# Beta as one table of 128 rows of 12 numbers: one load in place of three, one set of gate instructions in place of two

## The chip, the cores and the metric

The kernel runs on one core of a Trainium2 chip. The metric is the device time of one execution in microseconds (us); lower is better. A core has a matrix engine (PE, whose weight loads are shown apart as PEld), a vector engine (DVE), a scalar engine (ACT), a general engine (POOL) and a queue engine (SP), which here only issues DMAs. 16 DMA engines move the data between device memory (DRAM) and the core's on-chip memory, which has 128 rows called partitions.

## The reference

Four batches, eight heads, 576 positions, head size 64. Attention with a causal mask is mixed, by a gate for each head, with a read from a memory matrix; the result, 2304 tokens of 512 numbers, goes through a two-layer network with a squared ReLU.

```
scores = q @ k.T / sqrt(D), causal;  a = softmax(scores);  local = a @ v
q_p = phi(q)                              # phi(x) = (x if x > 0 else exp(x) - 1) + 1
mem_out = (q_p @ M_prev) / (q_p @ z_prev + 1e-6)
g = 1 / (1 + exp(-beta))                  # beta: one number for each of the 8 heads
attn = g * mem_out + (1 - g) * local
out = relu(x @ w_in) ** 2 @ w_out         # x: attn as [2304, 512]; w_in 512x2048, w_out 2048x512
```

The inputs arrive in 64-bit floats for the two weight matrices and in 32-bit floats for the rest. The host may lay inputs out anew; it does no arithmetic.

## The kernel before, in words

The whole program is one stream of work for each engine. A scheduler that runs while the program is built orders the instructions of every engine; the source fixes what depends on what, and the order is written out by the scheduler, so a change in one place can move instructions in others.

**First tokens.** `first_tokens` (L229) computes the attention output of positions 0 to 63 of all four batches, in two groups `g` of two batches. The list `SEQ` (L56) says in which order SP issues the loads of this stage: `a0` and `b0` (L250, L252, L254: q, k, rows of q, and z for group 0, into `tr`), `g` (`load_beta`, L116, which also emits the gate arithmetic), `a1` (group 1), `r` (one weight load, L197, into `raw`), `b1`, `r`, `c0` (L258: v and M for group 0), `l` (the loads of the first attention pair, L340, L344, L347), `r`, `r`, `c1`.

All these DMAs sit in one queue. Eight completion semaphores are used in rotation, so that from the ninth on each DMA is held back until the one issued eight places earlier has landed.

**Beta.** Before the change, `gp` has four columns: partitions 0 to 63 hold the even heads, partitions 64 to 127 the odd heads, so L117 and L118 each read four numbers that lie two apart in DRAM, for 64 partitions. `gm` has all eight heads on all 128 partitions (L119). `gates` (L127) forms 1/(1+exp(-beta)) in both tiles by an exponential on ACT (L129), an addition (L130) and a reciprocal (L131) on DVE for each; then come `gi`, `gm` as 1/(1-g), `gs`, `gpb` and `g1b` on DVE (L132 to L139). `gpb` and `g1b` are used by the first tokens (L283, L298), `gi`, `gm` and `gs` by the attention that follows (L438, L528, L410).

**phi of a group** (L271 to L284): exponential on ACT (L276), minimum on DVE (L277), then L278, L279, L280 to L283 on DVE, and L284 on POOL.

**Weights.** Each 512 KB piece of weights is loaded as raw 64-bit words into one of a few buffers (L197), turned into two 32-bit parts by L167, L169 and L173 on DVE with L168 and L172 on ACT between them (`split_weight`), and kept on chip.

**The rest.** `attention` (L350) works on pairs of heads; `moe` (L607) takes a block of 256 tokens, multiplies by `w_in` into `up` (L631 to L633) and by `w_out` into `oacc` (L621 to L623), each product in three parts. Attention of later pairs runs between the blocks of `moe`. The last stretch is `moe` alone.

Of the kernel before, what the change touches and what calls it, by code (L numbers as in the profile page):

```python
# [8 lines left out]
F32 = mybir.dt.float32  # L9
# [4 lines left out]
AF = mybir.ActivationFunctionType  # L14
ALU = mybir.AluOpType
AX = mybir.AxisListType

B, H, S, D = 4, 8, 576, 64
NP = H // 2
DM, FF = 512, 2048  # L20
NTOK = B * S
P = 128
# [68 lines left out]
def fused_kernel(ctx: ExitStack, tc: tile.TileContext, t0_d, zt_d, kk_d, qv_d, beta, w_in, w_out, out):  # L91
    nc = tc.nc
    w_in = w_in.bitcast(U32)
    w_out = w_out.bitcast(U32)
    cp = ctx.enter_context(tc.tile_pool(name="cp", bufs=1))
# [13 lines left out]
    nc.gpsimd.affine_select(  # L109
        out=mask, in_=mask, pattern=[[-1, MW]], compare_op=ALU.is_ge, fill=-1e30, base=448, channel_multiplier=1  # L110
    )
    gp = cp.tile([P, NP], F32, name="gp")
    gm = cp.tile([P, H], F32, name="gm")
    b2 = beta.rearrange("(p h) -> h p", h=2)

    def load_beta():  # L116
        nc.sync.dma_start(gp[:D], b2[0].partition_broadcast(D))  # L117
        nc.sync.dma_start(gp[D:], b2[1].partition_broadcast(D))  # L118
        nc.sync.dma_start(gm, beta.partition_broadcast(P))  # L119
        gates()  # L120

    gi = cp.tile([P, H], F32, name="gi")
# [2 lines left out]
    g1b = cp.tile([P, GN], F32, name="g1b")  # L125

    def gates():  # L127
        for t in (gp, gm):
            nc.scalar.activation(t, t, AF.Exp, scale=-1.0)  # L129
            nc.vector.tensor_scalar(out=t, in0=t, scalar1=1.0, scalar2=None, op0=ALU.add)  # L130
            nc.vector.reciprocal(t, t)  # L131
        nc.vector.reciprocal(gi, gm)  # L132
        nc.vector.tensor_scalar(out=gm, in0=gm, scalar1=-1.0, scalar2=1.0, op0=ALU.mult, op1=ALU.add)
        nc.vector.reciprocal(gm, gm)
        nc.vector.tensor_scalar(out=gs, in0=gm, scalar1=SC, scalar2=None, op0=ALU.mult)

        for b in range(GB):
            nc.vector.tensor_copy(gpb[:, b * NP : (b + 1) * NP], gp)
        nc.vector.tensor_scalar(out=g1b, in0=gpb, scalar1=-1.0, scalar2=1.0, op0=ALU.mult, op1=ALU.add)  # L139
# [89 lines left out]
    def first_tokens(tp, ahead):  # L229
# [10 lines left out]
        for step in SEQ.split():  # L240
            if step == "r":
                ahead()
            elif step == "l":
                nxt.append(loads(*order[0]))
            elif step == "g":
                load_beta()
            else:
                g = int(step[1])
                if step[0] == "a":
                    nc.sync.dma_start(tr[g][:, : 2 * GD], t0_d[g, :, : 2 * GD])  # L250
                elif step[0] == "b":
                    nc.sync.dma_start(tr[g][:, 2 * GD : 3 * GD], t0_d[g, :, 2 * GD : 3 * GD])  # L252
                    for h in range(2):
                        nc.sync.dma_start(  # L254
                            tr[g][h * D : (h + 1) * D, 3 * GD : 4 * GD], zt_d[2 * g + h].partition_broadcast(D)
                        )
                else:
                    nc.sync.dma_start(tr[g][:, 4 * GD :], t0_d[g, :, 3 * GD :])  # L258
# [525 lines left out]
```

## Time and profile before

| what | us |
|---|---|
| three runs, median | 615.64 |
| three runs, lowest and highest | 613.45 and 617.97 |
| the profiled execution, its own time | 613.01 |
| its span, first to last instruction | 611.2 |

The span is the part of the profiled execution that the trace covers; 1.81 us of its own time lie around it. Times of single instructions and waits come from this one execution and are counted from the span's start. An idle time in square brackets behind an instruction is how long its engine stood still before it, with what ended the wait.

### The profile page before, as it was taken

The numbers are of one execution on the slowest core, as the hardware profiler recorded it, in microseconds if no ns is written. First come the engines' busy times: TensorE is split into PE (matmuls) and PEld (weight loads), VectorE is DVE, ScalarE is ACT, GpSimd is POOL, SyncE is SP. The second block draws the span as 40 slices with busy tenths as digits, with TensorE's granted clock in tenths as the row PEclk, the third lists the DMA queues.
The fourth block names the chain that finished last, engine by engine and source line by source line (L and its number), as shares of the span: only waits on it lengthen the run. The fifth ranks groups of instructions, "written<-read, shape, count | busy, mean of one in ns | idle before, by whom it ended". The sixth has DMA issues, their size and how long they took to land.

```text
span 611.2 us, 11532 instructions
## 1 busy us (share of the span) xinstructions
PE 566.8 (93%) x4198; PEld 483.2 (79%) x4198; DVE 408.5 (67%) x1287; ACT 329.5 (54%) x748; POOL 168.8 (28%) x139
## 2 busy tenths in 40 slices
PE   2268999899998999999999999999999999999997
PEld 2156887688877887888888888888888899998996
DVE  3999989766878876977788989877787611001000
ACT  1598797565557645666565555654556412312312
POOL 1420213134432433133332333332421221221221
PEclk9995999999997999999999999999999999999999
DMA  5949476576465756585554755563536310200000
GB/s 180 394 154 373 118 222 161 128 168 132 99 125 134 174 108 125 126 194 131 131 131 102 153 120 147 124 162 92 119 83 118 88 34 1 69 1 1 35 0 35
DMA packets 128120, 76.28 MB, mean 125 GB/s; under 512 B 99904, under 2 KB 113216, under 8 KB 128064
## 3 DMA queue, kind: packets, MB, share of 16 engines
q1 hardware_dynamic: 128064, 75.55, 49.8%
q8 instruction: 33, 0.54, 0.4%
q14 instruction: 23, 0.19, 0.1%
HBM read 42.63 MB, written 8.78 MB: 84 GB/s over the span
## 4 chain that ended last, share of the span: by engine, by line
PE 67%; DVE 14%; DMA 12%; ACT 3%; issue 2%; SPq 1%; POOL 0%; ACTq 0%; DVEq 0%
PE up L631 10%; PE up L633 9%; PE up L632 9%; PE oacc L621 9%; PE oacc L622 8%; PE oacc L623 8%; PE sp L468 6%; DMA aT<-a 4%; DMA vv<-in_qv_dram 3%; DVE w L173 2%; PE acc L553 2%; PE pm L435 2%; DMA raw<-in_w_in_dram 2%; DVE a L523 2%; DVE e L472 1%
## 5 line engine op out<-in xcount | busy, mean ns | idle before, releaser
L631 PE MATMUL up<-xh,w 128*128 128x256 f32 x576 | 167.3, 291 | 0.2 <-DVE vy L409 0.2
L633 PE MATMUL up<-xh,w 128*128 128x256 f32 x576 | 166.1, 288 | 0.0
L632 PE MATMUL up<-xl,w 128*128 128x256 f32 x576 | 165.9, 288 | 0.0
L646 POOL TENSOR_TENSOR gl<-r,gh 128x512 fp32r<-128x512 f32 x72 | 100.7, 1398 | 222.6 <-DVE gh L645 125.8
L631 PEld LDWEIGHTS up<-xh,w 128*128 128x128 f32 x576 | 111.0, 193 | 8.6 <-issue 4.4
L621 PE MATMUL oacc<-w,gh 128*128 128x512 f32 x288 | 115.4, 401 | 0.0
L632 PEld LDWEIGHTS up<-xl,w 128*128 128x128 f32 x576 | 111.0, 193 | 5.1 <-issue 2.6
L633 PEld LDWEIGHTS up<-xh,w 128*128 128x128 f32 x576 | 110.9, 193 | 4.5 <-issue 3.3
L622 PE MATMUL oacc<-w,gh 128*128 128x512 f32 x288 | 114.0, 396 | 0.0
L484 ACT ACTIVATE e<-e,mx 128x320 f32<-128x320 f32 (+3 forms) x128 | 77.9, 610 | 62.6 <-DVE mx L472 62.5
L623 PE MATMUL oacc<-w,gl 128*128 128x512 f32 x288 | 109.3, 394 | 0.0
L637 ACT ACTIVATE r<-up 128x512 f32<-128x512 f32 x72 | 42.6, 592 | 118.3 <-PE up L633 113.1
L639 POOL TENSOR_TENSOR r<-r 128x512 f32<-128x512 f32 x40 | 45.4, 1134 | 153.8 <-ACT r L637 153.8
L523 DVE SCALAR_TENSOR_TENSOR a<-e,a 128x128 f16<-128x128 f32 x120 | 72.3, 623 | 14.8 <-ACT a L521 14.7
L645 DVE CAST gh<-r 128x512 fp32r<-128x512 f32 x40 | 17.0, 425 | 90.1 <-ACT r L641 87.9
L472 DVE CUSTOM_DVE_ANT_0 e<-sp,mask 128x320 f32<-128x320 f32 (+3 forms) x128 | 56.6, 475 | 8.9 <-PE sp L468 8.6
L621 PEld LDWEIGHTS oacc<-w,gh 128*128 128x128 f32 x288 | 54.3, 188 | 10.4 <-issue 0.7
L622 PEld LDWEIGHTS oacc<-w,gh 128*128 128x128 f32 x288 | 54.3, 189 | 9.4 <-issue 1.0
L623 PEld LDWEIGHTS oacc<-w,gl 128*128 128x128 f32 x288 | 53.1, 188 | 10.8 <-issue 0.6
L521 ACT ACTIVATE a<-e 128x128 f16<-128x128 f32 x120 | 56.9, 521 | 1.5 <-DMA aT<-a 0.8
L553 PE MATMUL acc<-vs,aT 128*128 128x128 f16 x308 | 37.1, 220 | 0.0
L555 DVE TENSOR_REDUCE s<-acc 128x128 f32<-128x256 f32 x60 | 24.2, 417 | 18.3 <-PE acc L553 18.3
(130 smaller groups left out, 885.3 us busy)
## 6 DMA issues: line engine op xcount, KB each, us to landing
raw<-in_w_in_dram SPq DMA_DIRECT2D x11, 512.0 KB, 8.7
vv<-in_qv_dram SPq DMA_DIRECT2D x16, 320.0 KB, 3.1
raw<-in_w_out_dram SPq DMA_DIRECT2D x9, 512.0 KB, 7.1
kd<-in_kk_dram SPq DMA_DIRECT2D x16, 288.0 KB, 3.1
out_dram<-o SPq DMA_DIRECT2D x16, 256.0 KB, 2.4
xd<-memx SPq DMA_DIRECT2D x31, 128.0 KB, 2.1
xn<-xd SPq DMA_DIRECT2D x14, 256.0 KB, 2.8
qm<-in_qv_dram SPq DMA_DIRECT2D x8, 321.0 KB, 3.1
```

The costliest lines, as they stand in the source:

```text
L472: nc.vector.tensor_tensor_reduce(out=e[:n, h, ks], in0=sps[:n, h, :w], in1=mask[:n, 448 - q0 + s * w : 448 - q0 + s * w + w], scale=-0.125 ...
L484: nc.scalar.activation(e[:n, h, :ke], e[:n, h, :ke], AF.Exp, bias=bs, scale=-1.0, accum_out=sm[:n, h : h + 1])
L521: nc.scalar.mul(av[:, :, o0 : o0 + w], x, SC)
L523: nc.vector.scalar_tensor_tensor(out=av[:, :, o0 + w : o0 + 2 * w], in0=x, scalar=SC, in1=av[:, :, o0 : o0 + w], op0=ALU.mult, op1=ALU.sub ...
L553: nc.tensor.matmul(o2, aT[:, h * nb + c, :n], vs[:, h, c], start=False, stop=c == i)
L621: nc.tensor.matmul(acc[t], gh[:, u, ts], w_out_op(f, 0), start=f == 0, stop=False)
L622: nc.tensor.matmul(acc[t], gh[:, u, ts], w_out_op(f, 1), start=False, stop=False)
L623: nc.tensor.matmul(acc[t], gl[:, u, ts], w_out_op(f, 0), start=False, stop=f == NF - 1)
L631: nc.tensor.matmul(up[:, u, :], w_in_op(f, k, 0), xh[:, k, :], start=k == 0, stop=False)
L632: nc.tensor.matmul(up[:, u, :], w_in_op(f, k, 0), xl[:, k, :], start=False, stop=False)
L633: nc.tensor.matmul(up[:, u, :], w_in_op(f, k, 1), xh[:, k, :], start=False, stop=k == NK - 1)
L646: nc.gpsimd.tensor_tensor(out=gl, in0=r, in1=gh.bitcast(F32), op=ALU.subtract)
```

## The change

The host lays beta out as a table of 128 rows of 12 numbers: four for `gp` (even heads in rows 0 to 63, odd heads in rows 64 to 127) and eight for `gm`. One DMA loads the table into the tile `gpm`, of which `gp` and `gm` are now column ranges. Exponential, addition and reciprocal run once over the 12 columns. What follows in `gates` is as before.

```diff
-    gp = cp.tile([P, NP], F32, name="gp")
-    gm = cp.tile([P, H], F32, name="gm")
-    b2 = beta.rearrange("(p h) -> h p", h=2)
+    gpm = cp.tile([P, NP + H], F32, name="gpm")
+    gp, gm = gpm[:, :NP], gpm[:, NP:]
 
     def load_beta():
-        nc.sync.dma_start(gp[:D], b2[0].partition_broadcast(D))
-        nc.sync.dma_start(gp[D:], b2[1].partition_broadcast(D))
-        nc.sync.dma_start(gm, beta.partition_broadcast(P))
+        nc.sync.dma_start(gpm, beta)
         gates()
...
     def gates():
-        for t in (gp, gm):
-            nc.scalar.activation(t, t, AF.Exp, scale=-1.0)
-            nc.vector.tensor_scalar(out=t, in0=t, scalar1=1.0, scalar2=None, op0=ALU.add)
-            nc.vector.reciprocal(t, t)
+        nc.scalar.activation(gpm, gpm, AF.Exp, scale=-1.0)
+        nc.vector.tensor_scalar(out=gpm, in0=gpm, scalar1=1.0, scalar2=None, op0=ALU.add)
+        nc.vector.reciprocal(gpm, gpm)
         nc.vector.reciprocal(gi, gm)
...
+    bt = _np.asarray(inputs["beta"])
+    bt = _np.concatenate([_np.repeat(bt.reshape(NP, 2).T, D, axis=0), _np.tile(bt, (P, 1))], axis=1)
...
-        "beta": _np.ascontiguousarray(inputs["beta"]),
+        "beta": _np.ascontiguousarray(bt),
```

Lines behind the change have lower numbers afterwards: by 3 from L119 to L116, by 4 from L130 on. The scheduler writes the order anew; three places follow.

SP's queue at the start of the program, before. `tr` are the loads of the first tokens, `raw` the weights; the numbers behind names only tell buffers apart.

```order
L250 DMA tr_119<-in_t_dram 128x1024
L252 DMA tr_119<-in_t_dram 128x512
L254 DMA tr_119<-in_zt_dram 64x512 x2
L117 DMA gp<-in_beta_dram 64x4x1
L118 DMA gp<-in_beta_dram 64x4x1
L119 DMA gm<-in_beta_dram 128x8
L250 DMA tr_120<-in_t_dram 128x1024
L197 DMA raw_142<-in_w_in_dram 128x1024
L252 DMA tr_120<-in_t_dram 128x512
L254 DMA tr_120<-in_zt_dram 64x512 x2
```

The same place after the change:

```order
L246 DMA tr_118<-in_t_dram 128x1024
L248 DMA tr_118<-in_t_dram 128x512
L250 DMA tr_118<-in_zt_dram 64x512 x2
L116 DMA gpm<-in_beta_dram 128x12
L246 DMA tr_119<-in_t_dram 128x1024
L193 DMA raw_136<-in_w_in_dram 128x1024
L248 DMA tr_119<-in_t_dram 128x512
L250 DMA tr_119<-in_zt_dram 64x512 x2
```

Three DMAs of beta have become one at the same place in the queue; what stands around it is in the same order.

DVE at the gates, before (`w` and `t` belong to phi of group 0, L278 to L283):

```order
L130 TENSOR_SCALAR gp<-gp 128x4
L278 SCALAR_TENSOR_TENSOR w<-tr_119,w 128x8x64
L131 RECIPROCAL gp<-gp 128x4
L130 TENSOR_SCALAR gm<-gm 128x8
L279 TENSOR_TENSOR tr_119<-tr_119,w 128x512
L138 COPY gpb<-gp 128x4 x2
L131 RECIPROCAL gm<-gm 128x8
L280 TENSOR_REDUCE t_179<-tr_119 128x8
L139 TENSOR_SCALAR g1b<-gpb 128x8
...
L283 TENSOR_TENSOR t_179<-t_179,gpb 128x8
L135 TENSOR_SCALAR gs<-gm 128x8
L167 TENSOR_SCALAR raw_142<-raw_142 128x512
```

The same after the change (rows in the middle of either piece are left out, the same arithmetic in both):

```order
L126 TENSOR_SCALAR gpm<-gpm 128x12
L274 SCALAR_TENSOR_TENSOR w<-tr_118,w 128x8x64
L127 RECIPROCAL gpm<-gpm 128x12
L275 TENSOR_TENSOR tr_118<-tr_118,w 128x512
L128 RECIPROCAL gi<-gpm 128x8
L134 COPY gpb<-gpm 128x4 x2
L276 TENSOR_REDUCE t_173<-tr_118 128x8
...
L163 TENSOR_SCALAR raw_136<-raw_136 128x512
L278 RECIPROCAL t_173<-t_173 128x8
L131 TENSOR_SCALAR gs<-gpm 128x8
L279 TENSOR_TENSOR t_173<-t_173,gpb 128x8
```

One addition and one reciprocal are gone, the addition on beta is still ahead of L278 (L274 after the change), and the first weight piece's L167 (L163) now stands three short instructions earlier.

SP's queue later, while the last weights are loaded (`xw` and `hw` are weight pieces in borrowed buffers, `xd` and `aT` belong to attention), before:

```order
L197 DMA raw_677<-in_w_in_dram 128x1024
L574 DMA xd_92<-memx 128x2x128
L197 DMA xw<-in_w_out_dram 128x512
L197 DMA hw<-in_w_in_dram 128x1024
L197 DMA xw<-in_w_out_dram 128x512
L527 DMA_TRANSPOSE aT<-a 128x6x128
L197 DMA hw<-in_w_in_dram 128x1024
L340 DMA kd<-in_kk_dram 128x576
```

And after the change:

```order
L570 DMA xd_91<-memx 128x2x128
L193 DMA raw_671<-in_w_in_dram 128x1024
L193 DMA xw<-in_w_out_dram 128x512 x2
L523 DMA_TRANSPOSE aT<-a 128x6x128
L193 DMA hw<-in_w_in_dram 128x1024 x2
L340 DMA qm<-in_qv_dram 128x130
L340 DMA qm<-in_qv_dram 128x256
L336 DMA kd<-in_kk_dram 128x576
```

The same DMAs are there, and their order has changed: the store of `xd` is one weight piece earlier, both `xw` pieces come ahead of the transpose, and `kd` behind `qm`. From there on the order differs at many places, on PE, DVE and ACT too.

## Rows read from the trace of the kernel before

**Rows 1.** From the profile's page: busy time of the engines over the whole span; then the granted clock of PE in tenths of full speed, and the data rate, in 40 slices of 15.3 us.
```profile
PE 566.8 (93%) x4198; PEld 483.2 (79%) x4198; DVE 408.5 (67%) x1287; ACT 329.5 (54%) x748; POOL 168.8 (28%) x139
...
PEclk9995999999997999999999999999999999999999
...
GB/s 180 394 154 373 118 222 161 128 168 132 99 125 134 174 108 125 126 194 131 131 131 102 153 120 147 124 162 92 119 83 118 88 34 1 69 1 1 35 0 35
```

**Rows 2.** The chain of waits that ends at 80 us, two of its steps: start, length, what.
```profile
5.37 10.10 DMA raw<-in_w_in_dram
15.49 0.98 DVE raw L167
```

**Rows 3.** The DMA view of 0 to 13 us in 40 slices of 0.325 us, with the packets by size.
```profile
GB/s 0 0 0 0 0 101 113 176 239 365 403 410 403 391 347 177 95 7 0 0 0 1 0 0 0 1 1 0 13 14 27 40 92 216 354 391 372 442 416 403
DMA packets 1383, 1.95 MB, mean 150 GB/s; under 512 B 771, under 2 KB 771, under 8 KB 1383
```

**Rows 4.** The DMA view of 5.6 to 8.6 us.
```profile
DMA packets 306, 0.00 MB, mean 1 GB/s; under 512 B 305, under 2 KB 305, under 8 KB 306
```

**Rows 5.** The DMA issues of SP in order of time: start, length, engine, line, what, count.
```profile
2.89 0.65 SPq L117 DMA_DIRECT2D gp<-in_beta_dram  x1
3.59 0.62 SPq L118 DMA_DIRECT2D gp<-in_beta_dram  x1
4.25 0.61 SPq L119 DMA_DIRECT2D gm<-in_beta_dram  x1
4.89 0.43 SPq L250 DMA_DIRECT2D tr<-in_t_dram  x1
5.37 0.44 SPq L197 DMA_DIRECT2D raw<-in_w_in_dram  x1
5.85 1.77 SPq L252 DMA_DIRECT2D tr<-in_t_dram  x1
7.67 2.70 SPq L254 DMA_DIRECT2D tr<-in_zt_dram  x2
```

**Rows 6.** From issue to landing of the two DMAs of `gp`, from the view of that tile.
```profile
DMA to landing us min/median/max: 4.9/6.4/7.8
```

**Rows 7.** The engines in order of time, 6 to 16 us, the instructions around the gates; the idle time before and what ended it in brackets.
```profile
6.13 0.43 DVE L277 TENSOR_SCALAR w<-w 128x512 f32<-128x512 f32 x1 [3.33 <-ACT w L276]
...
11.48 0.20 ACT L129 ACTIVATE gp<-gp 128x4 f32<-128x4 f32 x1 [5.38 <-DMA gp<-in_beta_dram]
11.72 0.17 DVE L130 TENSOR_SCALAR gp<-gp 128x4 f32<-128x4 f32 x1 [5.16 <-ACT gp L129]
...
12.51 0.21 ACT L129 ACTIVATE gm<-gm 128x8 f32<-128x8 f32 x1 [0.83 <-DMA gm<-in_beta_dram]
12.75 0.17 DVE L130 TENSOR_SCALAR gm<-gm 128x8 f32<-128x8 f32 x1 [0.17 <-ACT gm L129]
12.86 0.69 DVE L279 TENSOR_TENSOR tr<-tr,w 128x512 f32<-128x512 f32 x1
...
13.82 1.97 PE L269 MATMUL sp<-tr 64*64 64x64 f32 x32 [7.36 <-DMA tr<-in_t_dram]
...
15.02 0.17 DVE L135 TENSOR_SCALAR gs<-gm 128x8 f32<-128x8 f32 x1
15.49 0.97 DVE L167 TENSOR_SCALAR raw<-raw 128x512 uint32<-128x512 uint32 x1 [0.30 <-DMA raw<-in_w_in_dram]
```

**Rows 8.** The longest waits of DVE between 15.4 and 57.9 us: what waited, for what, us in total, times, the longest.
```profile
DVE w L173 <- ACT w L172: 0.6, 1, 0.6
DVE raw L167 <- DMA raw<-in_w_in_dram: 0.3, 1, 0.3
```

**Rows 9.** Stretches of the program: length, busy us of PE, PEld, DVE, ACT and POOL (with counts), granted clock of PE as a share of full speed, DMA share, GB/s.
```profile
15.50:57.90 42.40, 22.68 (x155) 16.13 (x151) 41.20 (x106) 32.16 (x75) 11.44 (x10) 0.87 0.79 301
57.90:100.00 42.10, 41.86 (x270) 35.83 (x268) 39.44 (x108) 34.56 (x83) 10.10 (x7) 0.97 0.70 192
100.00:120.00 20.00, 16.52 (x112) 12.73 (x111) 16.56 (x61) 12.40 (x27) 3.41 (x3) 1.00 0.50 121
...
170.00:190.00 20.00, 17.19 (x126) 12.84 (x122) 16.27 (x63) 12.27 (x39) 4.66 (x5) 0.92 0.63 147
186.60:193.50 6.90, 6.73 (x32) 5.80 (x32) 6.45 (x28) 4.19 (x13) 0.00 (x0) 0.51 0.60 133
190.00:490.00 300.00, 297.15 (x2326) 253.37 (x2327) 242.13 (x791) 174.96 (x407) 89.64 (x71) 0.99 0.58 127
490.00:611.20 121.20, 117.71 (x767) 106.72 (x766) 12.05 (x27) 29.90 (x50) 26.61 (x21) 1.00 0.06 20
46.70:60.30 13.60, 10.79 (x43) 8.88 (x44) 12.50 (x38) 10.81 (x28) 0.84 (x1) 0.50 1.00 383
```

**Rows 10.** PE in order of time at the first product with `w_in`, two successive matmuls of one shape at the lower clock and two at the full clock.
```profile
59.95 0.41 PE L631 MATMUL up<-xh,w 128*128 128x256 f32 x1
60.16 0.41 PE L632 MATMUL up<-xl,w 128*128 128x256 f32 x1
...
67.02 0.28 PE L632 MATMUL up<-xl,w 128*128 128x256 f32 x1
67.14 0.28 PE L633 MATMUL up<-xh,w 128*128 128x256 f32 x1
```

## The prediction

> **What bounds the kernel now.** I read the page first. PE is busy 93% of the span, but its clock is down in the fourth of the 40 slices and partly in the thirteenth, and in the first five slices the data rate goes up and down [rows 1]. So the end is set by PE, and the start by something else. The cut by stretches shows where one passes into the other: from 15.5 to 57.9 us PE is busy 22.7 of 42.4 us and DVE 41.2; from 57.9 to 100 us PE is busy 41.9 of 42.1 us, and up to 490 us it stands still for few us in all [rows 9]. The change lies ahead of both, in the first 15.5 us. Whether a gain there reaches the end depends on two things: what ends those 15.5 us, and whether DVE, from there to 57.9, waits for anything that doesn't move with it.
>
> The chain of waits answers the first: it enters DVE's work at 15.49 with the first weight piece, which was issued at 5.37 and took 10.10 us to land [rows 2]. The DMA view shows why so long. The bytes of group 0 of the first tokens flow at some 400 GB/s up to about 5 us, then the rate falls to nothing for over 3 us and is back at 350 only at about 11 us [rows 3]. In that hole the queue is not empty: from 5.6 to 8.6 us 306 packets went through, 305 of them under 512 B [rows 4]. Those are beta. By the shapes in SP's order it is read as 2 x 64 x 4 single numbers (they lie two apart in DRAM) and 128 rows of 32 B, 640 packets in all; the whole of 0 to 13 us has 771 small ones [rows 3]. Behind beta, in the same queue, stand the loads of group 1 (issued at 4.89) and the first weight piece (5.37) [rows 5], and they get no bytes until beta is through. SP itself is held up too: the next issues take 1.77 us, and 2.70 us for two [rows 5].
>
> The time line of the engines shows the second victim. DVE is done with L277 at 6.56 and then stands still 5.16 us for the exponential of `gp`, whose data landed only at 11.48; `gm` came at 12.51, and the gates and the phi of group 0, mixed, last until L135 ends at 15.19. PE waits 7.36 us for group 1 [rows 7].
>
> **The change, part by part.**
>
> *The loads.* 640 packets become 128, one for each row of 48 B. In the hole they pass at 305 / 3.0 us = 102 per us [rows 4]. 640 of them make 6.3 us, 128 make 1.3 us; the queue behind them moves forward by 5.0 us. The rows have no packet of 48 B; bounds: the second half of `gp` (256 packets) landed at 3.59 + 7.8 = 11.4 and the first at 2.89 + 4.9 = 7.8 [rows 5, 6], so at the slowest of the 16 DMA engines 256 packets took 3.6 us, and a gain below 3.6 would mean that not even one of the three DMAs was saved; above, 6.3 if the new rows pass for nothing beside the bytes of group 0. Below that stands the case in which the hole isn't made by the packets at all (a rival, below). I take 5.0, since it comes from the hole itself.
>
> The row says that three small DMAs hold a queue for over 6 us. The Trainium skill (DMA: Bandwidth & Descriptors, "Anatomy of one DMA — SWDGE (gpsimd) path") speaks against it: about 2 us of a DMA are fixed and mostly completion, descriptor generation is small, and "You can emit a lot of descriptors before the incremental cost shows up". By that rule the three DMAs overlap and dropping two of them gives next to nothing, the rival below that leaves the hole open. The trace disagrees so far, with 4.9 and 7.8 us to landing for 1 KB each [rows 6]; the page's figure was fitted for the gpsimd path, and these come from SP.
>
> *SP.* From 2.89 to 4.89 the three issues take 2.0 us [rows 5]; one takes about 0.7, so group 1 is issued some 1.3 us sooner. That adds nothing to the 5.0: its bytes would still wait behind beta. If the hole were gone altogether, it would be the 1.3 us that count. The DMAs held back until the eighth before them has landed move with the landings.
>
> *Gates.* One exponential (0.21 us on ACT), one addition and one reciprocal on DVE go. ACT stood still 0.83 us before that exponential, so it is worth nothing. On DVE a short instruction holds the next back by 0.11 us (12.75 to 12.86) [rows 7]: 0.2 us for two. What the 12 columns cost over 4 or 8 I set at nothing: 4 and 8 columns took 0.17 us alike. A loss is here too: `gp` no longer comes 1.0 us ahead of `gm`; the first addition waits for all 12 columns, with L278 and the rest of phi queued behind it on DVE. So beta is there at 12.5 - 5.0 = 7.5, the addition starts 0.24 later as before (11.48 to 11.72), at 7.75, and the mixed work of 15.19 - 11.72 = 3.47 us, less 0.2, ends at 11.0. The first weight piece is there by 15.49 - 5.0 = 10.5; its L167 now stands three short instructions earlier, which lets it use some of that. DVE reaches its weight work at about 11.0 in place of 15.49: 4.5 us sooner. Late next is thus DVE, by 0.5 us, and no longer the data.
>
> *From 15.5 to 57.9 us.* DVE's longest waits there are 0.6 and 0.3 us [rows 8], so the stage is as long as DVE's work, which stays the same. It moves as a whole, and the first product with `w_in` goes from 57.9 to 53.4 us. From there PE carries the 4.5 us to the end.
>
> *The order.* The scheduler moves DMAs on SP while the last weights come in, and much on PE and DVE behind that. No row prices it. The nearest are the idle times that PE has in this order: 20.0 - 16.5 = 3.5 us at 100 to 120, 20.0 - 17.2 = 2.8 us at 170 to 190 [rows 9]. An order may save one of them or add one; I take nothing, with 2.8 to 3.5 us either way.
>
> *The sum.* The profiled execution took 613.01 us (span 611.2, 1.81 around it): 613.0 - 4.5 = 608.5. The median of the runs lies 2.6 above that execution, so 615.6 - 4.5 = 611.1, 0.7% less.
>
> **Rivals.**
>
> The low clock stays where it is. PE runs at half (1.2 GHz) from 46.7 to 60.3 us, after a stretch in which it was often idle [rows 9]. At that clock matmuls of 256 columns follow each other at 0.21 us (59.95 to 60.16), at the full 2.4 GHz at 0.12 us (67.02 to 67.14) [rows 10]. If the stretch doesn't move with the work, the 4.5 us of products that now come before 57.9 are done at that pace and lose 4.5 x (1 - 0.12 / 0.21) = 1.9 us: 613.0. For it: nothing shows what starts the stretch to the us. Against it: PE's idle time ahead of it moves with the work.
>
> The hole stays: it has another cause than the number of packets, or 128 rows of 48 B hold the queue as long. Then only 0.2 us go: 615.4. For it: the bytes moved are few in both. Against it: the 305 small packets in the hole, and that nothing else went through it.
>
> A better order. One of PE's idle times goes, and the low clock that follows it: from 186.6 to 193.5 us the granted clock is 0.51 [rows 9], which costs 6.9 x (1 - 0.12 / 0.21) = 3.0 us at PE's pace, with the 2.8 us of standing still 5.8. That gives 605.3. For it: such a fall comes only behind idle time, and the order is new. Against it: at 100 to 120 PE stood still longer and the clock stayed at 1.00, so the two needn't go together.
>
> A worse order, and the time is over 615.6. The place is where attention of a later pair stands in PE's queue ahead of products that could run, as at 170 to 190. One such stop more with its fall of the clock costs the same 5.8 us: 616.9. It decides from 4.5 us on, so a stop without the fall doesn't do it, and two with it give 622.7. For it: PE, DVE and SP are in a new order from about 70 us on. Against it: from 190 to 490 us PE stands still for only 2.9 us in 300 [rows 9], so there is much other work to put between.
>
> **How the numbers follow.** 1% of 615.64 is 6.2 us, about what a measurement of this kernel can tell from no change: faster is below 609.5, slower above 621.8. The forecast has 0.46, the low clock that stays 0.12, the hole that stays 0.10, the better order 0.20, the worse 0.12 (half of it two stops). Faster takes the better order and 0.12 of the forecast, where the gain of the loads is nearer to 6.3 or the order helps by a us or two: 0.32. Slower takes the two stops and 0.01 from the edge: 0.07. The same has the remaining 0.61. The predicted time is 611.1. The range goes from 604.5, below the better order, to 617.5, above one stop more; outside are the two stops and the edges of the order. The forecast's own range is 608 to 614.
>
> **What would show it.** Right: the data rate shows no hole of over 2 us between 5 and 11 us; beta lands near 7.5; the addition on beta starts near 7.8; the first weight piece is split from about 11.0 on; DVE is busy from there to the first product at about 53.4; the later stretches are as long as before within 3 us. Wrong: small packets still fill several us; or DVE is early by 4 us, but waits for data before 53; or the first product is early and the gain is gone by 200 us, with new idle time or a low clock on PE. The forecast fails above all if the later order gives or takes over 2 us.

## The result: 1.0% slower, with the start five us shorter

The changed kernel takes 622.88 us (median of 4 runs, 618.59 to 625.61), the kernel before 616.74 (median of 4 runs taken with them): a ratio of 1.0105, 95% interval 1.007 to 1.014. The forecast was 611.1 us, 604.5 to 617.5. It was wrong, and on the other side. The profiled execution of the changed kernel took 621.40 us against 613.01 before, 8.4 us more.

Its page, the same rows as in [rows 1] (busy time, granted clock and data rate in 40 slices, here of 15.5 us):

```profile
PE 571.1 (92%) x4198; PEld 484.9 (78%) x4198; DVE 409.8 (66%) x1285; ACT 330.2 (53%) x747; POOL 166.4 (27%) x139
...
PEclk9987999899998999999999999799999999999999
...
GB/s 297 374 194 247 222 178 139 122 105 133 111 146 106 144 94 164 97 169 134 154 93 151 109 112 86 149 137 116 103 82 112 83 111 10 68 1 1 35 0 35
```

The counts on PE are the same, DVE has two instructions fewer and ACT one, as the change says. The first slice moves 297 GB/s in place of 180. The granted clock has a fall that [rows 1] lack, a 7 in slice 26, near 390 us.

The start went as forecast, or better. The DMA view of 0 to 13 us, as in [rows 3], then that of 5.6 to 8.6 us, as in [rows 4]:

```profile
GB/s 0 0 0 0 0 101 139 139 277 429 391 353 391 403 391 207 226 191 252 315 366 391 391 366 378 359 359 353 252 284 277 303 290 277 334 277 391 403 429 389
DMA packets 1444, 3.60 MB, mean 277 GB/s; under 512 B 307, under 2 KB 313, under 8 KB 1444
...
DMA packets 296, 1.02 MB, mean 341 GB/s; under 512 B 26, under 2 KB 26, under 8 KB 296
```

The hole is not shorter, it is gone: the rate never falls below 190 GB/s after 3 us, and where 305 of 306 packets were small, 26 of 296 are. The same issues as in [rows 5], and the instructions that answer to [rows 7] (idle time before and its end in brackets):

```profile
2.89 0.59 SPq L116 DMA_DIRECT2D gpm<-in_beta_dram  x1
3.53 0.43 SPq L246 DMA_DIRECT2D tr<-in_t_dram  x1
4.00 0.43 SPq L193 DMA_DIRECT2D raw<-in_w_in_dram  x1
...
6.45 0.21 ACT L125 ACTIVATE gpm<-gpm 128x12 f32<-128x12 f32 x1 [0.64 <-DMA gpm<-in_beta_dram]
...
6.70 0.17 DVE L126 TENSOR_SCALAR gpm<-gpm 128x12 f32<-128x12 f32 x1 [0.42 <-ACT gpm L125]
...
9.90 0.43 DVE L163 TENSOR_SCALAR raw<-raw 128x512 uint32<-128x512 uint32 x1 [0.56 <-DMA raw<-in_w_in_dram]
...
52.53 0.56 PE L627 MATMUL up<-xh,w 128*128 128x256 f32 x1
```

Group 1 is issued at 3.53 in place of 4.89. The exponential starts at 6.45 (11.48 and 12.51 before), DVE takes up the first weight piece at 9.90 (15.49 before), and the first product with `w_in` starts at 52.53 (57.88 before): 5.35 us sooner.

So the 8.4 us, and the 5.35 on top of them, are lost behind 52.5 us. To find the place I mark the first copy out of `oacc` of each of the nine blocks of `moe`; the lengths between the marks, in us, in the profiled executions:

| kernel | start to first product | block 1 | 2 | 3 | 4 | 5 | 6 | 7 | 8 and 9 |
|---|---|---|---|---|---|---|---|---|---|
| before | 57.9 | 70.1 | 77.8 | 63.3 | 66.0 | 64.2 | 65.4 | 54.0 | 88.2 |
| changed | 52.5 | 73.4 | 78.0 | 63.9 | 64.7 | 75.6 | 59.4 | 59.5 | 88.2 |

Blocks 5 to 7 take 183.6 us before and 194.5 after. Block 1 has 3.3 us too; but that is the execution of before: the nine other profiles in before's order (e1, e3 to e6, e9, e10, e15 and e16 below) have 72.3 to 73.9 there. Its 613.01 us was a good draw, 3.7 below the median. Late in block 5 the changed kernel has a stop that before has not. Its steps on the chain of waits (start, length, what), then PE in order of time:

```profile
387.50 0.41 DVE memx L559 x2
387.90 0.02 issue
387.92 2.43 DMA xd<-memx
390.35 0.02 issue
390.37 2.59 DMA xn<-xd
392.96 0.04 issue
393.00 1.42 PE px L594 x8
```
```profile
390.12 0.23 PE L544 MATMUL acc<-vs,aT 128*128 128x128 f16 x1 [1.41 <-DMA aT<-a]
...
390.84 0.42 PE L464 MATMUL sp<-kh,qh 64*128 64x320 f32 x2
393.00 1.42 PE L594 MATMUL px<-identr,xn 128*128 128x128 f32 x8 [1.74 <-DMA xn<-xd]
```

The last rows of an attention are stored to `xd` and fetched back as `xn` for the next block, 5.0 us of two DMAs in a row; PE has run out of other work by then. It stands still for 1.41 us for the transposed `aT` and for 1.74 us for `xn`, and from 391.8 to 398.6 us the granted clock is 0.51, the 1.2 GHz level (columns as in [rows 9]):

```profile
391.80:398.60 6.80, 5.60 (x28) 5.05 (x29) 4.83 (x15) 4.66 (x11) 0.00 (x0) 0.51 0.32 111
```

All five further profiles in this order (e2, e11 to e14) have the same two waits there, of 1.5 to 1.8 and 1.8 to 3.1 us, and a fall of the clock beside them.

### The profile page after: what moved, and what is told of

Read it like the earlier page. It is cut to its first block, busy times and chain, and to the rows that moved or that the text cites. A ratio compares the mean times of both kernels' runs of the same rounds, so it can differ in the third digit from the quotient of the medians.

```text
span 619.6 us, 11535 instructions
## 1 busy us (share of the span) xinstructions
PE 571.1 (92%) x4198; PEld 484.9 (78%) x4198; DVE 409.8 (66%) x1285; ACT 330.2 (53%) x747; POOL 166.4 (27%) x139
## 4 chain that ended last, share of the span: by engine, by line
PE 55%; DVE 5%; DMA 4%; issue 1%; ACT 1%; POOL 0%; SPq 0%; ACTq 0%; DVEq 0%; POOLq 0%
PE up L627 8%; PE up L628 8%; PE up L629 8%; PE oacc L617 7%; PE oacc L619 7%; PE oacc L618 7%; PE sp L464 5%; DMA aT<-a 3%; PE acc L549 2%; PE pm L431 1%; DVE a L519 1%; PE acc L546 1%; PE acc L544 1%; PE px L594 1%; DVE memx L559 1%
## 5 line engine op out<-in xcount | busy, mean ns | idle before, releaser
L642 POOL TENSOR_TENSOR gl<-r,gh 128x512 fp32r<-128x512 f32 x72 | 99.4, 1381 | 217.7 <-DVE gh L641 133.1
L619 PE MATMUL oacc<-w,gl 128*128 128x512 f32 x288 | 110.9, 399 | 0.0
L519 DVE SCALAR_TENSOR_TENSOR a<-e,a 128x128 f16<-128x128 f32 x120 | 81.4, 693 | 27.7 <-ACT a L517 27.5
L633 ACT ACTIVATE r<-up 128x512 f32<-128x512 f32 x72 | 42.6, 592 | 100.2 <-PE up L629 92.7
L635 POOL TENSOR_TENSOR r<-r 128x512 f32<-128x512 f32 x40 | 43.4, 1085 | 171.6 <-ACT r L633 165.7
```

Source lines behind the costliest of these rows:

```text
L519: nc.vector.scalar_tensor_tensor(out=av[:, :, o0 + w : o0 + 2 * w], in0=x, scalar=SC, in1=av[:, :, o0 : o0 + w], op0=ALU.mult, op1=ALU.sub ...
L619: nc.tensor.matmul(acc[t], gl[:, u, ts], w_out_op(f, 0), start=False, stop=f == NF - 1)
L642: nc.gpsimd.tensor_tensor(out=gl, in0=r, in1=gh.bitcast(F32), op=ALU.subtract)
```

## Experiments

All ratios are to the kernel before, run on the same chip, with 95% intervals. "Old order" is that of the kernel before on PE, ACT and POOL, instruction for instruction but for the gates; "new order" that of the changed kernel. The code pieces leave out the host's lines, which lay beta out as the text says.

### One load, old order (e1), and the new order with many small reads (e2)

The first question was whether the loads or the order made it slower. In e1 two loads of 16 B into unused tiles follow the load of beta, so that beta takes three places in the queue again, and with that the scheduler writes the old order.

```diff
+    dum = [cp.tile([1, NP], F32, name=f"dum{i}") for i in range(2)]
     def load_beta():
         nc.sync.dma_start(gpm, beta)
+        for i in range(2):
+            nc.sync.dma_start(dum[i], beta[:1, :4])
```

> The changed kernel (table of 128 rows of 12 numbers, one load into gpm, gates once over 12 columns) with two loads of 16 B each added behind it into tiles that nothing reads, so that beta again takes three places in SP's queue. With them the scheduler gives PE, ACT (but for the one exponential) and POOL the order of the kernel before, instruction for instruction, and DVE the same but for the gates. Theory A (the short hole gives its gain, the new later order takes it and more): first product with w_in at about 52.5 us as in the changed kernel, later stretches as before, time 5 us under the kernel before, ratio 0.991. Rival B (the earlier start itself does the harm, since later transfers and attention meet differently): time near that of the changed kernel, ratio 1.01.

Measured: 614.04 us (12 runs), ratio 0.9937 (0.9914 to 0.9959). The table in one load makes the kernel faster; two loads that carry nothing turn 1% slower into 0.6% faster. The order is what costs; that it isn't the one load by itself, e8 below shows.

The second kernel keeps the new order and was to bring the hole back, with four runs of 12 B for each row, 512 packets.

```diff
-        nc.sync.dma_start(gpm, beta)
+        nc.sync.dma_start(gpm.rearrange("p (r c) -> p r c", r=4), beta.rearrange("p (r c) -> p r c", r=4)[:, :, :3])
```

> The changed kernel with the table laid out with a gap behind every three numbers, so that the one load takes 4 runs of 12 B per row: 512 packets in place of 128, near the 640 of before. The order on PE, ACT and POOL is that of the changed kernel, instruction for instruction. Theory A: the hole of the kernel before comes back (384 packets more at 102 per us are 3.8 us), the later order stays the bad one: 3 to 4.5 us above the changed kernel, ratio to the kernel before 1.015 to 1.018. Rival B (the earlier start does the harm): with the late start back, near the kernel before, ratio 1.00.

Measured: 624.28 us (6 runs), 1.0112 (1.0077 to 1.0147), and the hole did not come back. Its DMA view of 5.6 to 8.6 us and the landing of beta (us from issue to landing are the last number):

```profile
DMA packets 217, 0.81 MB, mean 271 GB/s; under 512 B 17, under 2 KB 17, under 8 KB 217
...
gpm<-in_beta_dram SPq DMA_DIRECT2D x1, 6.0 KB, 3.6
```

512 packets land in 3.6 us, the changed kernel's 128 in 3.5. The number of packets, on which the forecast's 5.0 us rest, makes no hole by itself. The time is that of the changed kernel, as it must be if only the order differs from e1.

### Gates alone (e3), and three loads of the table (e4)

e3 is the kernel before with its three loads going into one tile and the gate arithmetic merged; e4 has before's gates, and three loads that read the table, 256 packets of 16 and 32 B. Both run in the old order.

```diff
 # e4
-        nc.sync.dma_start(gp[:D], b2[0].partition_broadcast(D))
-        nc.sync.dma_start(gp[D:], b2[1].partition_broadcast(D))
-        nc.sync.dma_start(gm, beta.partition_broadcast(P))
+        nc.sync.dma_start(gp[:D], beta[:D, :NP])
+        nc.sync.dma_start(gp[D:], beta[D:, :NP])
+        nc.sync.dma_start(gm, beta[:, NP:])
```

> The second half of the change alone: the three loads of the kernel before, now into column ranges of gpm, and the gates once over 12 columns. PE, ACT (but for the exponential) and POOL in the order of before. Both A and B: one exponential, one addition and one reciprocal go beside a DVE that waits for beta anyway, but phi's first instructions now wait for gm too (1.0 us); the first weight piece is not there before 15.5 us, which hides it: ratio 1.000, within 0.002. If the merged gates were a cause of the loss: ratio above 1.005.

Measured: 617.78 us (12 runs), 1.0018 (0.9992 to 1.0044). Merging the gates is worth nothing. With three loads the merged exponential waits for all of them: it starts at 12.80, the first product at 58.42.

> Only the packets: beta from the table by three loads (64 rows of 16 B, 64 rows of 16 B, 128 rows of 32 B, 256 packets in place of 640) into gp and gm; gates as before. Order of all engines as before. Theory A: 384 packets fewer at 102 per us make the hole 3.8 us shorter, and the gates start earlier by that: 3.5 to 4 us under the kernel before, ratio 0.994, between e1 and the kernel before. Rival B: no gain or a loss, ratio 1.00 to 1.01.

Measured: 612.44 us (9 runs), 0.991 (0.9879 to 0.9941). More than expected: the exponentials start at 6.91 and 7.02, the first product at 52.48, and there is no hole either. The whole gain of the change lies in where beta is read from, neither in the number of DMAs nor in the gates.

### What makes the hole (e5, e6, e9, e10)

e2 and e4 say that it isn't the packets' number. In before, every partition reads the same few bytes; in the table each has its own. e5 has before's three loads, with before's shapes and its 640 packets, but beta is repeated 128 times in memory and each partition reads its own row. In e6 all partitions read the same places, in runs of 16 and 32 B, 256 packets; of its lines and of e9's, only the new ones are shown.

```diff
 # e5
-    b2 = beta.rearrange("(p h) -> h p", h=2)
+    b2 = beta.rearrange("q (p h) -> h q p", h=2)
...
-        nc.sync.dma_start(gp[:D], b2[0].partition_broadcast(D))
-        nc.sync.dma_start(gp[D:], b2[1].partition_broadcast(D))
-        nc.sync.dma_start(gm, beta.partition_broadcast(P))
+        nc.sync.dma_start(gp[:D], b2[0, :D])
+        nc.sync.dma_start(gp[D:], b2[1, D:])
+        nc.sync.dma_start(gm, beta)
 # e6
+        nc.sync.dma_start(gp[:D], beta[:NP].partition_broadcast(D))
+        nc.sync.dma_start(gp[D:], beta[NP:H].partition_broadcast(D))
+        nc.sync.dma_start(gm, beta[H:].partition_broadcast(P))
```

> The kernel before with beta as a table of 128 equal rows: the three loads have the shapes of before (64 x 4 single numbers, 64 x 4 single numbers, 128 rows of 32 B, 640 packets), but each partition reads its own row of DRAM, where before all partitions read the same 32 B. Order on all engines as before. E2 sent 512 packets of 12 B, each from its own place, and had no hole, so the count alone isn't it. Theory H1 (single numbers of 4 B are slow to read): the hole stays, the gates' exponentials near 11.5 and 12.5 us, time as before, ratio 1.00. Theory H2 (64 or 128 reads of the same DRAM place are slow): the hole goes, exponentials near 7 us, ratio 0.992.

> The other half: beta as 16 numbers in DRAM (even heads, odd heads, all heads), so that the three loads read whole runs of 16, 16 and 32 B, but all partitions the same ones (256 packets). Order on all engines as before. H1: no single numbers, no hole, exponentials near 7 us as with the table in e4, ratio 0.991. H2: 256 packets that read the same place at 102 per us, 2.5 us: exponentials near 9 us and ratio 0.994 to 0.996.

Measured: e5 611.22 us (10 runs), 0.9908 (0.9884 to 0.9931); e6 611.60 (10 runs), 0.9924 (0.9889 to 0.9958). In e5 there is no hole, with single numbers two apart as before: the DMA view of 5.6 to 8.6 us, then ACT in order of time.

```profile
DMA packets 454, 0.78 MB, mean 261 GB/s; under 512 B 263, under 2 KB 263, under 8 KB 454
```
```profile
6.88 0.21 ACT L129 ACTIVATE gp<-gp 128x4 f32<-128x4 f32 x1 [0.50 <-DMA gp<-in_beta_dram]
```

Beside 263 small packets 191 large ones pass, at 261 GB/s. In e6 the 256 reads of the same few places cost little: its exponentials start at 6.79 and 7.58, the second 0.6 later than e5's 6.99, where slow reads of one place (H2) had them near 9. So one place alone doesn't make it either; it takes many reads of it. e9 and e10 take one each: e9 has runs of 8 B for all, 768 packets from the same places; e10 has `gp` as before (512 single numbers from the same places) and `gm` from own rows.

```diff
 # e9
+    b3 = beta.rearrange("(r c) -> r c", c=3)[:, :2]
+        nc.sync.dma_start(gp[:D].rearrange("p (r c) -> p r c", c=2), b3[:2].partition_broadcast(D))
+        nc.sync.dma_start(gp[D:].rearrange("p (r c) -> p r c", c=2), b3[2:4].partition_broadcast(D))
+        nc.sync.dma_start(gm.rearrange("p (r c) -> p r c", c=2), b3[4:].partition_broadcast(P))
 # e10
-    b2 = beta.rearrange("(p h) -> h p", h=2)
+    b2 = beta[:H].rearrange("(p h) -> h p", h=2)
...
-        nc.sync.dma_start(gm, beta.partition_broadcast(P))
+        nc.sync.dma_start(gm, beta[H:].rearrange("(p h) -> p h", h=H))
```

> The kernel before with beta as 16 numbers in DRAM with a gap behind every second one: the three loads read runs of 8 B, 128 + 128 + 512 = 768 packets, all partitions from the same few places. Order on PE, ACT and POOL as before. E5 (640 packets of 4 and 32 B, own rows) and E2 (512 of 12 B, own rows) had no hole, e6 (256 of 16 and 32 B, same places) only some 0.6 us for gm. Theory H2' (many reads of one place are slow, at 102 per us): a hole as long as before or longer, exponentials of gp near 8 and of gm near 12 us or later. Theory H1' (it needs single numbers of 4 B and the same place together): exponentials near 7 to 8 us, no hole.

> The kernel before with gm from a table of 128 equal rows (own rows), gp as before: 512 single numbers of 4 B, all from the same 32 B of DRAM. Order on all engines as before. H2': 512 reads of one place at 102 per us are 5.0 us: exponential of gp near 11, of gm right behind it; the hole a little shorter than before. H1': the same. If neither (the 128 reads of gm from the same 32 B had made the hole): exponentials near 7 to 8 us.

Measured, one run each beside one of before at 617.79: 616.89 and 617.12 us. Both have the hole. e9's DMA view of 5.6 to 8.6 us and its two exponentials:

```profile
DMA packets 348, 0.01 MB, mean 4 GB/s; under 512 B 343, under 2 KB 343, under 8 KB 348
```
```profile
7.15 0.20 ACT L129 ACTIVATE gp<-gp 128x4 f32<-128x4 f32 x1 [0.75 <-DMA gp<-in_beta_dram]
...
13.06 0.21 ACT L129 ACTIVATE gm<-gm 128x8 f32<-128x8 f32 x1 [5.70 <-DMA gm<-in_beta_dram]
```

and e10's:

```profile
DMA packets 246, 0.00 MB, mean 0 GB/s; under 512 B 246, under 2 KB 246, under 8 KB 246
```
```profile
11.64 0.20 ACT L129 ACTIVATE gp<-gp 128x4 f32<-128x4 f32 x1 [5.78 <-DMA gp<-in_beta_dram]
```

In e10 the 512 reads are alone enough; e9's `gp` with its 256 reads is early, and ACT then waits 5.7 us for its `gm` with 512. Reads of the same place pass at 343 / 3.0 = 114 per us for 8 B and 246 / 3.0 = 82 for 4 B (102 in [rows 4]), and next to nothing else gets through the queue meanwhile. The same shapes from own rows (e5 against before) make no hole.

### Without the stop (e7), and a third order (e8)

e7 is the changed kernel, but the block behind the stop fetches rows of another batch that were stored long before, and so works on other tokens; the order is the changed kernel's up to there and is written anew behind it. e8 has one load of the table, with the gates in two passes over its column ranges; it comes out in a third order: in the traces, 2512 of PE's 4198 matmuls stand at the same place in the queue as in the new order and 1635 as in the old.

```diff
 # e7
-            nc.sync.dma_start(src.bitcast(F32)[:, : nk * P], xd[b][r0 : r0 + P, : nk * P])
+            nc.sync.dma_start(src.bitcast(F32)[:, : nk * P], xd[1 if (b, blk) == (2, 0) else b][r0 : r0 + P, : nk * P])
 # e8
-        nc.scalar.activation(gpm, gpm, AF.Exp, scale=-1.0)
-        nc.vector.tensor_scalar(out=gpm, in0=gpm, scalar1=1.0, scalar2=None, op0=ALU.add)
-        nc.vector.reciprocal(gpm, gpm)
+        for t in (gp, gm):
+            nc.scalar.activation(t, t, AF.Exp, scale=-1.0)
+            nc.vector.tensor_scalar(out=t, in0=t, scalar1=1.0, scalar2=None, op0=ALU.add)
+            nc.vector.reciprocal(t, t)
```

> The changed kernel, in which the sixth block of 256 tokens (batch 2, first half) fetches its inputs from the rows of batch 1 instead of batch 2: its computation is on the wrong tokens, and its fetch no longer waits for the store of attention that had landed 2.4 us after its issue. Order as in the changed kernel up to the fourth block, changed behind it. Theory A1 (in the new order PE stands at 385 to 398 us for this fetch, 3.2 us, and its clock falls from 391.8 to 398.6, 3.0 us): the time falls by 5 to 8 us, to 615 to 618, ratio to before 0.997 to 1.002. Rival A2 (the stop only shows what is late anyway; attention on DVE bounds that stretch): it stays within 2 us of the changed kernel, ratio 1.008 or more.

> The one load of 128 rows into gpm, but exponential, addition and reciprocal run apart over its 4 and its 8 columns as before. The scheduler makes a third order of it (four fifths of PE's instructions stand as in the changed kernel, half as before). Theory A (the loss belongs to one order, not to one load): first product at 52 to 53.5 us as in the changed kernel, and the end anywhere between 610 and 623; nearer to the changed kernel's, 619 to 623, if the shared parts hold the stop at 385 to 398 us. Rival B (an early start harms in any order) is out since e1; a rival here is that one load always costs: 622 or more.

Measured: e7 619.01 us (10 runs), 1.003 (0.9994 to 1.0066); e8 617.57 (10 runs), 1.0008 (0.9982 to 1.0035). The stop, with what the order behind it changes, is worth 622.9 - 619.0 = 3.9 us by the medians, 4.6 by the ratios (the two were not run side by side); it isn't all. Three orders of the same work, each with the early start, give 614.0 (e1), 617.6 (e8) and 622.9.

Where the rest is shows in a cut by stretches: blocks 1 to 4, block 5, blocks 6 and 7; length, then busy us of PE with its count of matmuls first. e1 (old order, no hole):

```profile
53.10:333.24 280.14, 270.44 (x2001) 226.07 (x2000) 228.96 (x729) 179.19 (x419) 81.62 (x65) 0.98 0.60 139
333.24:397.28 64.04, 64.04 (x521) 55.15 (x520) 56.80 (x187) 36.18 (x88) 19.20 (x16) 1.00 0.62 136
397.28:516.87 119.59, 118.34 (x904) 103.27 (x903) 71.23 (x228) 55.54 (x124) 31.89 (x24) 1.00 0.40 88
```

The changed kernel:

```profile
52.53:332.49 279.96, 264.19 (x1962) 220.77 (x1961) 220.37 (x704) 172.94 (x405) 81.47 (x65) 0.98 0.59 136
332.49:408.06 75.57, 72.42 (x550) 60.88 (x549) 58.85 (x182) 41.43 (x98) 21.99 (x18) 0.95 0.50 114
408.06:526.96 118.90, 118.90 (x912) 102.80 (x911) 76.48 (x258) 56.48 (x127) 28.17 (x22) 1.00 0.44 96
```

And e7:

```profile
53.07:334.20 281.13, 264.54 (x1963) 221.98 (x1962) 220.05 (x703) 173.10 (x405) 79.61 (x65) 0.98 0.59 136
334.20:398.43 64.23, 64.23 (x494) 53.71 (x493) 51.82 (x162) 35.15 (x79) 20.22 (x16) 1.00 0.53 118
398.43:524.28 125.85, 124.66 (x968) 107.55 (x967) 84.03 (x278) 62.32 (x145) 29.99 (x24) 1.00 0.47 100
```

Blocks 1 to 4 take the same 280 us, but in the new order PE does 39 matmuls (2001 less 1962) and 6.25 us less in them: it stands still for 15.8 us there, in the old order for 9.7. What it didn't do then (26 of the 39 belong to attention, 13 to the network) it does in blocks 5 to 7, where PE has nothing to give: in the old order it is idle for 1.25 of 183.6 us there. e7, which has no stop, shows this part alone: 16.6 us idle in blocks 1 to 4, 494 + 968 matmuls behind them in place of 521 + 904, and 190.1 - 183.6 = 6.45 us more. The stop, with what the order behind it changes, adds 194.5 - 190.1 = 4.4. Together that is 10.8 us, where the two profiled executions differ by 10.2 (the first product is 0.57 us earlier in the changed kernel's).

The other profiles bear this out. In the ten of the old order PE does 2001 or 2002 matmuls in blocks 1 to 4 and is idle there for 8.3 to 11.2 us; in the six of the new order, and in e7, it does 1962 or 1963 and is idle for 15.0 to 18.7. e8's order lies between, with 1986 matmuls and 13.6 us, and its blocks 5 to 7, without the stop, take 186.7 us. One thing more varies: in the new order blocks 1 to 4 themselves take from 279.0 us (e2) to 287.0 (e12), in the nine old ones beside before 279.8 to 282.2. That may be why the new order costs a little more than 10.8 us in the medians below.

Why PE stands still more in blocks 2 and 3 is in its longest waits, here of the changed kernel from 125.9 to 267.8 us (what waited, for what, us in total, times, the longest), which in e1 sum to 1.1 for `xn` and hold no `DVE s`:

```profile
PE px L594 <- DMA xn<-xd: 2.9, 1, 2.9
PE vt L400 <- DVE s L551: 1.9, 1, 1.9
PE acc L544 <- DMA aT<-a: 1.9, 2, 1.1
```

Again a fetch of `xn` behind a store of `xd` leads: 2.9 to 3.4 us in all profiles of the new order, 1.1 to 2.3 in the old. These waits were not taken away one by one, so that they are the cause is argued and not shown.

### The four cells (e11 to e16)

With the cause of the hole known, the new order can be had with the hole: after's order, all partitions reading the same 12 numbers in four runs of 12 B, 512 reads (the odd heads' partitions thus take the even heads' gates, and only the time counts). e12 is the changed kernel beside it.

```diff
 # e11, against the changed kernel
-        nc.sync.dma_start(gpm, beta)
+        nc.sync.dma_start(gpm.rearrange("p (r c) -> p r c", r=4), beta.rearrange("(r c) -> r c", r=4)[:, :3].partition_broadcast(P))
```

> The changed kernel, its one load in 4 runs of 12 B per row as in e2, but all partitions read the same row of DRAM: 512 reads of one place (the gates of the odd heads' partitions in the first tokens then take the even heads' numbers). Order on PE, ACT and POOL as in the changed kernel. Theory A with what e9 and e10 showed (some 100 reads of one place per us): the exponential near 10.5 to 11.5 us in place of 6.45, the first product 4.5 to 5 us later than in the changed kernel, and the end later by as much: 627 to 628, ratio to before 1.018. Rival B2 (in the new order the later stops absorb what the start gives): within 1.5 us of the changed kernel.

> The changed kernel itself on the chip of e11, to compare the two there. As measured before: ratio to the kernel before 1.0105 (1.007 to 1.014), about 622 to 624.

Measured: e11 626.9 us (4 runs), 1.0171 (1.0129 to 1.0214); e12 627.09 (4 runs), 1.0158 (1.0113 to 1.0202). The hole is there (exponential at 12.64, first product at 59.23 against 52.09), and the two times tie. e12 itself lies above its expectation, at 1.0158 where the same kernel had 1.0105. The tie speaks against a start that counts; with four runs each, and intervals 0.9% wide, it doesn't settle it. So the same two were run with the two cells of the old order, e15 (the kernel of e1) and e16 (that of e3), side by side on one chip.

> New order with the hole (the kernel of e11). Theory A (order and start add up): 5 to 6 us above e14. Theory B3 (in the new order PE's later stops and falls of the clock take in what the start gives): within 2.5 us of e14.

> New order without the hole (the changed kernel). Ratio to the kernel before between the 1.0105 and 1.0158 of its two measurements. Theory A: 5 to 6 us below e13; B3: within 2.5 us of it.

> Old order without the hole (the kernel of e1). Both theories: 0.991 to 0.995 of the kernel before, 10 us under e14.

> Old order with the hole and the merged gates (the kernel of e3). Both theories: 1.000 to 1.003 of the kernel before, 4 to 5 us above e15.

Measured, with the kernel before beside them at 616.69 us (20 runs):

| | with the hole | without it | the hole costs |
|---|---|---|---|
| old order | e16: 616.51 us, 12 runs, 1.0002 (0.9977 to 1.0026) | e15: 612.14, 9 runs, 0.9928 (0.9902 to 0.9955) | 4.4 |
| new order | e13: 628.92, 6 runs, 1.0194 (1.0152 to 1.0237) | e14: 623.78, 5 runs, 1.0120 (1.0091 to 1.0148) | 5.1 |
| the new order costs | 12.4 | 11.6 | |

The two costs add up, within the noise (by the intervals, an estimate of 2 to 3 us in each difference). The tie of e11 and e12 I put down to scatter: e12's profile is the one with 287.0 us in blocks 1 to 4, where e11's has 281.6. The DMA view of 5.6 to 8.6 us in e13, with the landing of beta, against e2 above, which has the same 512 runs of 12 B from own rows:

```profile
DMA packets 248, 0.04 MB, mean 15 GB/s; under 512 B 238, under 2 KB 238, under 8 KB 248
...
gpm<-in_beta_dram SPq DMA_DIRECT2D x1, 6.0 KB, 8.7
```

One DMA of the same shape takes 8.7 us in place of 3.6 to land, for nothing but the place that it reads.

## Why the prediction was wrong

*The loads*: near in size by luck, wrong in the reason. I took 5.0 us from 640 packets at 102 per us [rows 4], with 1.3 us left for 128; the first weight piece came 5.6 us sooner, since nothing was left. But a packet's number or size costs nothing here (e5: all 640, no hole). What holds the queue is hundreds of reads of one and the same place in DRAM, and the table gives every row its own. The Trainium skill (DMA: Bandwidth & Descriptors, "Anatomy of one DMA — SWDGE (gpsimd) path"), which says that many descriptors can be emitted before they begin to cost, and which I had put against the hole and which speaks of the gpsimd path, holds on SP's queue for the reads of own rows (512 packets land in 3.6 us), and not for those of one place (8.7 us).

*SP and the gates*: right. Merging them is worth no time (e3), and the exponential started at 6.45 where I had 7.5, since no rest of the hole was left.

*From 15.5 to 57.9 us*: right. DVE bounds that stage and it moved as a whole, 42.4 us before and 42.6 after. The low clock moved with the work (46.7 to 60.3 before [rows 9], 40.2 to 53.9 after, in the row below with its columns), so the first rival didn't come. The term of 4.5 us measured 5.35 in the profiles, and 4.4 and 5.1 in the cells.

```profile
40.20:53.90 13.70, 10.61 (x41) 8.58 (x41) 12.99 (x39) 11.07 (x28) 1.06 (x1) 0.50 0.99 386
```

*The order*: this is the step that failed. I wrote "I take nothing, with 2.8 to 3.5 us either way", and it costs 11.6 to 12.4 us. With the old order kept, e1, e15 and e4 take 614.0, 612.1 and 612.4, where I had 611.1. The price was taken from the idle time of one place, as if an order could lose only there. And the argument against the worse order was read the wrong way round. PE's 297 busy us of 300 between 190 and 490 us [rows 9] were to mean that there is other work to put into a gap. They mean that a stretch that full can take in no work that was put off earlier: 39 matmuls that the old order did in the gaps of blocks 1 to 4 take 6.25 us of PE there, and when they came late they cost about all of it (6.45 in e7).

*The rivals*: the worse order was among them, with "622.7" for two stops, and 622.88 was measured; it had 0.06 of the chance, outside the range. That the number fits is chance, for its mechanism is half right: one stop with the fall of the clock is there, at 390 us, and costs 3.9 to 4.6 us (by the medians and the ratios; 4.4 in the profiles) where I had 5.8; the other 6.45 are work put off, which I did not think of. That the clock falls behind such a stop came as told: 0.51 from 391.8 on.

What stays open: why the scheduler comes to the new order when two DMAs go (with them back it returns to the old one, e1; with one load and the gates in two passes it comes to a third, e8), which of the waits in blocks 2 and 3 put the work off, why reads of one place in DRAM are slow, and why 512 of them cost some 5 us where 256 cost 0.6.

Versions that beat both kernels are e4, e5 and e6 (0.991, 0.9908 and 0.9924: three loads that don't read one place so often, in the old order) and e1, the change with two loads of 16 B that keep the order (0.9937, and 0.9928 when it was run again as e15).

## What to carry to other kernels

Where a scheduler writes the order, an edit that removes a DMA is two edits: price the order by itself, by keeping the number of queue entries with tiny loads, before a time is put down to the edit. PE's idle time is a place where work gets done; an order that wastes it in a loose stretch pays in the full ones, so compare busy time and counts stretch by stretch and not only the waits. Small values that all partitions need are better laid out once for each partition than read hundreds of times from one place.

## Not expected of the hardware

Where hundreds of small reads of the same place in DRAM stand in one queue, they pass at 79 to 114 per us (82 at 4 B in e10, 114 at 8 B in e9, 238 / 3.0 = 79 at 12 B in e13), and what stands behind them waits; 512 of them put the landing of one load from 3.6 to 8.7 us. 256, in e6, cost 0.6 us.
